# Two of twelve gate tiles add their sine product in the cosine's bank, with two ScalarE copies

## The chip, the cores and the metric

The kernel runs on one core of a Trainium2 chip. The metric is the device time of one launch in microseconds (us); lower is better. Engines are named as in the profile: PE is TensorE (PEld its weight loads), DVE is VectorE, ACT is ScalarE, POOL is GpSimd, and SP issues most of the transfers.

## The reference

```python
def _attn_ref(x):                       # x: (8, 3008, 256) float32
    X = np.fft.fft(x, axis=1)
    X = np.fft.fft(X, axis=2)
    return X.real.astype(np.float32)

def _moe_ref(x, w_gate, w_val, w_out):  # w_gate, w_val: (256, 1536), w_out: (1536, 256)
    gate = np.maximum(x @ w_gate, 0.0)
    val = x @ w_val
    return (gate * val @ w_out).astype(np.float32)
```

The real part of a two-dimensional Fourier transform of each of 8 batches (over 3008 positions and 256 channels) goes through a gated network: relu of the gate product, times the value product, times the output weights. The output is (24064, 256) in float32.

## The kernel before

**The mathematics.** The transform over the channels is folded into the weights: `WA` holds cosine combinations of the weights' rows and `WB` sine combinations (index 0 for the gate, 1 for the value). The transform over positions gives two matrices per batch, `U` (even part) and `V` (odd part), with one column for each pair of positions that mirror each other. For such a pair the gate is `WA·U + WB·V` at one position and `WA·U − WB·V` at the mirrored one; the same holds for the value. `WM` is `WB` times −2, so that adding `WM·V` to a bank that holds the sum turns it into the difference (the "mirror" matmul). Channel 128 does not fit into the 128 rows of the contraction. Its value stands in row 0 of `V`, and as a whole row in `CB`, spread over all partitions; row 0 of `WB` holds its weights, and row 0 of `WM` is zero. For the gates of batches 1 to 7 its term is therefore put into the bank ahead of the matmul by ScalarE: `CB` times a weight per partition, `b2`.

**Tiles and slots.** Batches 1 to 7 have three column blocks each (512, 512 and 481 columns), and each block has 12 tiles, one for each group of 128 of the 1536 features. A tile is a gate and a value for 128 features and one block of columns. The function `slot` emits the work of one tile step; it has tiles at four stages in hand: `pending` (the tile before), `cur`, `nxt` two tiles after `cur`, and `after` three tiles after it (the tile between, `mid`, waits). In a slot the kernel before emits:

- `sine_part(nxt)`: a matmul `WM[0]·V` into bank `g` (line 1015), and a ScalarE copy of it, `q`, to SBUF (line 1018);
- five of the eight output matmuls of the column block before (line 781; 128 × 256 each);
- `cosine_part(nxt)`: a matmul `WA[0]·U` added to the seeded bank `p` (line 1022);
- `seed(after)`: ScalarE writes `CB` times `b2` into a bank `p` (line 1010). There are two `p` banks, so this one was used by the tile two before it and must have been read by that tile's line 1026;
- the mirror matmul of `pending`'s value (line 880) and its second product on VectorE (line 910);
- the two value matmuls of `cur` (lines 874, 875) and its first product on VectorE (line 910: relu of the gate times the value, in one instruction);
- `both(nxt)`: VectorE makes the gate `sp = p − q/2` (line 1026), GpSimd the mirrored gate `sm = sp + q` (line 1027);
- GpSimd folds of a later batch, one evacuation, one sum (line 597) where there is one, and the remaining output matmuls. Some slots end with three matmuls of the next batch's position transform (line 585): by `DFT_EVEN`, slots 0 and 2 of every six in the first two column blocks, for batches that have a next one.

**What sets the order.** The program's order on every engine is written out by hand (`manual_schedule`): the order of these calls is the order in each engine's queue. Waits between engines come from the data and from the rotation of banks and buffers: one bank `g`, two each of `p`, `v` and `o`, one `d`, and 12 SBUF buffers `r` for gates.

**Around it.** Batch 0 runs in four narrower segments with other functions (`first_tile`, `single_tile`); in its first segment steps of `weights(c)` make the remaining columns of `WA` and `WB`. `gate_128` turns row 0 of `WB[0]` into the per-partition `b2` with twelve one-column matmuls (line 836) and a VectorE copy (line 837), in segment 2. At the end of batch 0 the first two tiles of batch 1 are begun ahead of time (`prime`, `seed`, `sine_part`, `cosine_part`, `both`). One tile of batch 1 (block 0, feature 6, kind "o") takes the older way with three gate matmuls and two ScalarE relus.

Of the kernel before, what the change touches and what calls it, by code (L numbers as in the profile page):

```python
# [11 lines left out]
F32 = mybir.dt.float32  # L12
BF16 = mybir.dt.bfloat16
I32 = mybir.dt.int32
F16 = mybir.dt.float16
ALU = mybir.AluOpType
ACTF = mybir.ActivationFunctionType
# [12 lines left out]
def dram(ap, offset, pattern):  # L30
    return bass.AP(ap.tensor, offset, [list(p) for p in pattern])
# [3 lines left out]
def kernel(  # L35
# [8 lines left out]
    nc = tc.nc  # L44
    B, S, D = x.shape
    DF = moe_w_gate.shape[1]
    NF = DF // 128
# [12 lines left out]
    psD = ctx.enter_context(tc.tile_pool(name="psD", bufs=1, space=PS))  # L60
    ctx.enter_context(tc.manual_schedule())

    def single(name, shape, dt=F32, pool=const):
        return pool.tile(shape, dt, name=name, tag=name)
# [4 lines left out]
    WB = [single(f"WB{i}", [128, DF], BF16) for i in range(2)]  # L69
    WM = [single(f"WM{i}", [128, DF], BF16) for i in range(2)]  # L70
# [349 lines left out]
    def weights(c):  # L420

        f = slice(c * 512, (c + 1) * 512)

        def one(i, T, W):
            p = psO.tile([128, 512], F32, name="o", tag="o")
            for kc in range(2):
                nc.tensor.matmul(p[:], lhsT=T[:, kc, :], rhs=wr[i][c][:, kc, :], start=(kc == 0), stop=(kc == 1))
            if (i, c, W) == (0, 1, WA):
                return lambda: nc.scalar.copy(W[i][:, f], p[:])
            if (i, W) in ((1, WA), (c - 1, WB)):  # L430
                nc.vector.tensor_scalar(W[i][:, f], p[:], scalar1=1.0, op0=ALU.mult, scalar2=None)  # L431
            else:
                nc.scalar.copy(W[i][:, f], p[:])
        return [lambda i=i, T=T, W=W: one(i, T, W) for i in range(2) for T, W in ((TA, WA), (TB, WB))]
# [22 lines left out]
    for t in range(3):  # L457
        n = ROWS[1][t]
        p = slice(0, n)
# [42 lines left out]
            nc.gpsimd.tensor_tensor(FF[0][p, 0, t, :, 0:1], even[:, :, 0:1], even[:, :, 0:1], op=ALU.add)  # L502
    start_pool.__exit__(None, None, None)
    ch128 = nc.dram_tensor("ch128", (B, 4 * NJ + 1), BF16, kind="Internal").ap()
    b2 = single("b2", [128, NF])
    one = single("one", [1, 1], BF16)
    nc.vector.memset(one[:], 1.0)


    def even_table(n, c):  # L510
# [311 lines left out]
    fold_even()  # L822
    turns_and_rows()

    more = {(0, i): [s] for i, s in enumerate(weights(1) + weights(2))}
    for n, c in enumerate(even_order):
        for k, step in enumerate(even_table(n, c)):
            more.setdefault(divmod(EVEN_AT[n] + k, NF), []).append(step)
# [1 line left out]
    for seg in (2, 3):  # L830
        more.setdefault((1, 8 + seg), []).append(lambda seg=seg: minus_v(nc.scalar, seg))

    def gate_128():
        p = psD.tile([128, 512], F32, name="d", tag="d")
        for f in range(NF):
            nc.tensor.matmul(p[:, f:f + 1], lhsT=WB[0][0:1, f * 128:(f + 1) * 128], rhs=one[:], start=True, stop=True)
        nc.vector.tensor_scalar(b2[:], p[:, 0:NF], scalar1=1.0, op0=ALU.mult, scalar2=None)
    more[(2, 2)] = [gate_128]
    more_1 = {}
    for at, step in zip((-5, -4, -3, -2, -1, 7, 7, 8, 14, 17), channel_loads() + channel_turn()):  # L840
        (more_1 if at >= 0 else more).setdefault(at if at >= 0 else (3, NF + at), []).append(step)

# [4 lines left out]
    todo_out, todo_dft, todo_fold = [], [], []  # L847
    credit, paired = 0, False
    pending = None

    def run(todo, n):
        for _ in range(min(n, len(todo))):
            todo.pop(0)()
        if not paired:
            flush()

    def run_one(todo):
        if todo:
            todo.pop(0)()
# [17 lines left out]
    def mirror(bank, st, i):  # L877

        W, v = (WB, st["vm"]) if st["b"] == 0 else (WM, st["vs"])
        nc.tensor.matmul(bank[:, 0:st["n"]], lhsT=W[i][:, st["f"]], rhs=v, start=False, stop=True, skip_group_check=True)  # L880

    def bank(tag):
        return {"g": psG, "p": psP, "v": psV, "d": psD}[tag].tile([128, 512], F32, name=tag, tag=tag)

    def space():
        return rp.tile([128, 512], F32, name="r", tag="r", bufs=12)

    def relu(st):
        st["r"] = space()
        nc.scalar.activation(st["r"][:, 0:st["n"]], st["g"][:, 0:st["n"]], ACTF.Relu)  # L890
# [6 lines left out]
    def mult(st, sign, r=None):  # L897
        n = st["n"]
        nc.vector.tensor_tensor(half_h(st, sign), (r or st["r"])[:, 0:n], st["v"][:, 0:n], op=ALU.mult)  # L899
# [8 lines left out]
    def relu_mult(st, sign):  # L908
        n = st["n"]
        nc.vector.scalar_tensor_tensor(half_h(st, sign), in0=st["s"][1 + sign][:, 0:n], scalar=0.0, in1=st["v"][:, 0:n],  # L910
                                       op0=ALU.max, op1=ALU.mult)

    def second(st):
        (relu_mult if "s" in st else mult)(st, 1)
        if st["n"] == 481:
            keep_rest(st)
# [5 lines left out]
    def value(st):  # L922
        st["v"] = bank("v")
        two(st["v"], st, 1)

    def gate(st, tag="g"):
        st["g"] = bank(tag)
        two(st["g"], st, 0)
        relu(st)
# [10 lines left out]
    def single_tile(st, outs, extra=(), last=(), tag="p"):  # L940

        gate(st, tag)
        if pending is not None:
            finish(pending)
        value(st)
        mult(st, 0)
        run(todo_out, outs)
        for step in extra:
            step()
        mirror(st["g"], st, 0)  # L950
        relu(st)
        run(todo_out, outs)
        for step in last:
            step()
        return st

    def first_tile(st, extra, outs):
# [31 lines left out]
    def new_tiles():  # L989
        for b in range(1, B):  # L990
            for blk, block in enumerate(thirds):
                for fi in range(NF):
                    st = tile_of(block, fi, uv[b])
                    st["b"] = b
                    st["kind"] = "o" if (b, blk, fi) == (1, 0, 6) else "n"
                    st["lead"] = (b, blk, fi) == (1, 0, 0)
                    yield st

    def prime():
# [4 lines left out]

    def seed(st, p=None):

        if st is None or st["kind"] == "o":
            return
        st["p"] = p or bank("p")
        nc.scalar.activation(st["p"][:, 0:st["n"]], st["c"], ACTF.Copy, scale=b2[:, st["fi"]:st["fi"] + 1])  # L1010

    def sine_part(st):
        n = st["n"]
        st["g"] = bank("g")
        nc.tensor.matmul(st["g"][:, 0:n], lhsT=WM[0][:, st["f"]], rhs=st["vs"], start=True, stop=True)  # L1015
        q = space()
        st["s"] = q, space(), q
        nc.scalar.copy(q[:, 0:n], st["g"][:, 0:n])  # L1018

    def cosine_part(st):  # L1020
        n = st["n"]
        nc.tensor.matmul(st["p"][:, 0:n], lhsT=WA[0][:, st["f"]], rhs=st["us"], start=False, stop=True, skip_group_check=True)  # L1022

    def both(st):
        n, (q, sp, sm) = st["n"], st["s"]
        nc.vector.scalar_tensor_tensor(sp[:, 0:n], in0=q[:, 0:n], scalar=-0.5, in1=st["p"][:, 0:n], op0=ALU.mult, op1=ALU.add)  # L1026
        nc.gpsimd.tensor_tensor(sm[:, 0:n], sp[:, 0:n], q[:, 0:n], op=ALU.add)  # L1027

    def slot(cur, mid, nxt, after, outs, fold_us):

        stop = len(todo_out)

        def out(part):
            run(todo_out, len(todo_out) - stop + outs * part // 8)
        old = nxt is not None and nxt["kind"] == "o"
        new = nxt is not None and not old
        if old:
            gate(nxt)
        lead = cur["lead"]
        if lead:  # L1040
            out(5)
        if new and mid["kind"] != "o":
            sine_part(nxt)
        out(3 if not lead else 5)
        out(5)
        if new and mid["kind"] == "o":
            sine_part(nxt)
        if new:
            cosine_part(nxt)
        seed(after)  # L1050
        if pending is not None:
            mirror(pending["v"], pending, 1)
        if pending is not None:
            second(pending)
        value(cur)
        if cur["kind"] == "o":
            mult(cur, 0, cur["first"])
        else:
            relu_mult(cur, 0)
        if new:  # L1060
            both(nxt)
        if old:
            nxt["first"] = nxt["r"]
            mirror(nxt["g"], nxt, 0)
            relu(nxt)
        run_fold(fold_us)
        run_one(evict)
        run_one(sums)
        out(8)
        return cur  # L1070
# [4 lines left out]
    for b in range(B):  # L1075
# [4 lines left out]
        for blk, block in enumerate(blocks):  # L1080
# [44 lines left out]
            if (b, blk) == (0, 0):  # L1125
                for fi in range(NF):
                    st = tile_of(block, fi, (U, V, CB))
                    add_h(st, hs)
                    if fi == 8:
                        todo_out = out_steps(b, block, hs, True)  # L1130
                    pending = first_tile(st, more.get((0, fi), ()), 6)
                mirror(pending["g"], pending, 0)
                relu(pending)
            elif not paired:
                for fi in range(NF):
                    st = tile_of(block, fi, (U, V, CB))
                    add_h(st, hs)
                    tag = {(3, 8): "g", (3, 9): "d", (3, 10): "g", (3, 11): "d"}.get((blk, fi), "p")
# [8 lines left out]
                    if (blk, fi) == (1, 8):  # L1147
                        run(todo_out, len(todo_out))
                        todo_out = out_steps(b, block, hs, True)
                    pending = single_tile(st, 3 if blk == 1 else per_tile // 2, more_b.get((blk, fi), ()), last, tag)  # L1150
                    run(todo_dft, DFT_0[blk - 1][fi])
            else:
                for fi in range(NF):
                    at = NF * blk + fi
                    cur = ahead.pop(0)
# [17 lines left out]
            if (b, blk) == (B - 1, 2):  # L1173
                todo_out = rest
# [38 lines left out]
```

## Time and profile before

| | us |
|---|---|
| median of 3 runs | 630.92 |
| lowest, highest | 630.84, 631.08 |
| the profiled execution | 630.98 |
| its span in the trace | 629.2 |
| busy: PE, DVE, ACT, POOL | 620.5, 551.5, 445.5, 502.7 |

The page names groups of instructions by the line of the kernel, the engine, the operation, and what is written from what. Ends of matmuls are modelled, because matmuls are pipelined: a 512-column matmul shows about 0.38 us although the next one starts 0.22 us later. Distances between starts are therefore the better measure on TensorE. A row of the timeline has the start, the duration (of all merged instructions, with their count at the end), and in brackets the engine's idle time ahead of it with its releaser. The clock of TensorE was granted in full all along.

### The profile page before, as it was taken

The numbers are of one execution on the slowest core, as the hardware profiler recorded it, in microseconds if no ns is written. First come the engines' busy times: TensorE is split into PE (matmuls) and PEld (weight loads), VectorE is DVE, ScalarE is ACT, GpSimd is POOL, SyncE is SP. The second block draws the span as 40 slices with busy tenths as digits, with TensorE's granted clock in tenths as the row PEclk, the third lists the DMA queues.
The fourth block names the chain that finished last, engine by engine and source line by source line (L and its number), as shares of the span: only waits on it lengthen the run. The fifth ranks groups of instructions, "written<-read, shape, count | busy, mean of one in ns | idle before, by whom it ended". The sixth has DMA issues, their size and how long they took to land.

```text
span 629.2 us, 12441 instructions
## 1 busy us (share of the span) xinstructions
PE 620.5 (99%) x4114; PEld 398.4 (63%) x4114; DVE 551.5 (88%) x981; ACT 445.5 (71%) x813; POOL 502.7 (80%) x478
## 2 busy tenths in 40 slices
PE   8999999999999999999999999999999999999997
PEld 2566666566666666666666666666666666666666
DVE  8886676999899899988999999899999989999991
ACT  7796667777777767777777777777777777777762
POOL 8887992898999988799979989699886566666660
PEclk9999999999999999999999999999999999999999
DMA  9953748734264327315362426211221111211113
GB/s 240 209 206 118 173 177 102 182 73 151 82 150 145 126 76 183 113 44 165 83 187 64 140 76 130 68 50 36 77 61 38 42 60 56 57 38 51 51 44 102
DMA packets 82911, 66.47 MB, mean 106 GB/s; under 512 B 38517, under 2 KB 65941, under 8 KB 82846
## 3 DMA queue, kind: packets, MB, share of 16 engines
q1 hardware_dynamic: 78260, 60.01, 34.3%
q0 software_dynamic: 3984, 4.92, 3.9%
q10 hardware_dynamic: 602, 0.75, 0.4%
q8 instruction: 32, 0.52, 0.4%
q14 instruction: 33, 0.27, 0.2%
HBM read 41.88 MB, written 34.16 MB: 121 GB/s over the span
## 4 chain that ended last, share of the span: by engine, by line
PE 91%; DVE 4%; issue 2%; POOL 1%; DMA 1%; ACT 1%; DVEq 0%; ACTq 0%; POOLq 0%
PE o L781 36%; PE v L880 10%; PE v L875 9%; PE v L874 9%; PE g L1015 8%; PE p L1022 8%; PE d L585 4%; DVE h L910 2%; PE p L880 1%; PE p L874 1%; PE p L875 1%; DMA XG<-in_x_dram,gidx 1%; DVE h L899 1%; DVE r L1026 1%; POOL XG L120 1%
## 5 line engine op out<-in xcount | busy, mean ns | idle before, releaser
L1027 POOL TENSOR_TENSOR r<-r 128x512 f32<-128x512 f32 (+1 forms) x251 | 313.2, 1254 | 100.5 <-DVE r L1026 98.1
L910 DVE SCALAR_TENSOR_TENSOR h<-r,v 128x512 bf16<-128x512 f32 (+1 forms) x502 | 317.1, 673 | 39.2 <-PE v L880 26.5
L781 PE MATMUL o<-wo,h 128*128 128x256 bf16 x2172 | 330.6, 272 | 0.0
L781 PEld LDWEIGHTS <-h 128*128 128x128 bf16 x2220 | 216.7, 98 | 112.0 <-issue 1.3
L1010 ACT ACTIVATE p<-CB,b 128x512 f32<-128x512 bf16 (+1 forms) x251 | 171.8, 684 | 73.4 <-DVE r L1026 72.1
L1018 ACT COPY r<-g 128x512 f32<-128x512 f32 (+1 forms) x251 | 145.1, 578 | 66.5 <-PE g L1015 57.4
L1026 DVE SCALAR_TENSOR_TENSOR r<-r,p 128x512 f32<-128x512 f32 (+1 forms) x251 | 167.9, 669 | 0.9 <-ACT r L1018 0.9
L875 PE MATMUL v<-V,WB 128*128 128x512 bf16 (+3 forms) x296 | 108.6, 367 | 0.0
L874 PE MATMUL v<-U,WA 128*128 128x512 bf16 (+3 forms) x296 | 108.6, 367 | 0.0
L880 PE MATMUL v<-V,WM 128*128 128x512 bf16 (+1 forms) x252 | 94.4, 375 | 0.8 <-DVE h L910 0.4
L1015 PE MATMUL g<-V,WM 128*128 128x512 bf16 (+1 forms) x251 | 94.1, 375 | 0.5 <-ACT r L1018 0.4
L1022 PE MATMUL p<-U,WA 128*128 128x512 bf16 (+1 forms) x251 | 94.1, 375 | 0.2 <-ACT p L1010 0.2
L899 DVE TENSOR_TENSOR h<-r,v 128x376 bf16<-128x376 f32 (+2 forms) x90 | 46.2, 546 | 17.6 <-PE v L880 10.1
L874 PEld LDWEIGHTS <-WA 128*128 128x128 bf16 x348 | 33.9, 97 | 39.5 <-issue 10.4
L875 PEld LDWEIGHTS <-WB 128*128 128x128 bf16 x348 | 34.0, 98 | 34.3 <-DVE WB L431 0.6
L794 ACT COPY os<-o 128x512 f32<-128x512 f32 x92 | 52.6, 571 | 3.5 <-issue 3.0
L198 POOL TENSOR_TENSOR XG<-XG,XD 128x510 f32<-128x510 f32 x42 | 53.0, 1270 | 0.8 <-DMA XG<-xr 0.8
L890 ACT ACTIVATE r<-p 128x376 f32<-128x376 f32 (+1 forms) x80 | 38.0, 486 | 17.8 <-PE p L880 9.0
L206 POOL TENSOR_TENSOR AA<-XG 128x510 f32<-128x510 f32 x42 | 45.5, 1093 | 0.0
L1015 PEld LDWEIGHTS <-WM 128*128 128x128 bf16 x251 | 24.6, 98 | 5.7 <-issue 0.3
L1022 PEld LDWEIGHTS <-WA 128*128 128x128 bf16 x251 | 24.5, 98 | 3.7 <-issue 0.8
L880 PEld LDWEIGHTS <-WM 128*128 128x128 bf16 x253 | 24.8, 98 | 3.1
(186 smaller groups left out, 412.3 us busy)
## 6 DMA issues: line engine op xcount, KB each, us to landing
out_dram<-os SPq DMA_DIRECT2D x124, 128.0 KB
xr<-in_x_dram SPq DMA_DIRECT2D x12, 768.0 KB
XG<-xr SPq DMA_DIRECT2D x12, 768.0 KB
XD<-in_x_dram SPq DMA_DIRECT2D x15, 512.0 KB
out_dram<-os SPq DMA_DIRECT2D x35, 112.0 KB
XD<-in_x_dram SPq DMA_DIRECT2D x8, 448.0 KB
CB<-ch SPq DMA_DIRECT2D x7, 376.2 KB
out_dram<-os SPq DMA_DIRECT2D x13, 96.0 KB
```

What stands on the lines that cost most here:

```text
L198: e.tensor_tensor(XG[p, r, t, ::-1, 1:D], XG[p, r, t, ::-1, 1:D], XD[p, r, t, :, D - 1:0:-1], op=ALU.add)
L781: nc.tensor.matmul(st["p"][0:m, q, :], lhsT=lhs(f), rhs=wo[:, f, :], start=(f == 0 and not (early and q)), stop=(f == NF - 1), skip_group_ ...
L874: nc.tensor.matmul(bank[:, 0:st["n"]], lhsT=WA[i][:, st["f"]], rhs=st["us"], start=True, stop=False)
L875: nc.tensor.matmul(bank[:, 0:st["n"]], lhsT=WB[i][:, st["f"]], rhs=st["vs"], start=False, stop=True)
L880: nc.tensor.matmul(bank[:, 0:st["n"]], lhsT=W[i][:, st["f"]], rhs=v, start=False, stop=True, skip_group_check=True)
L910: nc.vector.scalar_tensor_tensor(half_h(st, sign), in0=st["s"][1 + sign][:, 0:n], scalar=0.0, in1=st["v"][:, 0:n], op0=ALU.max, op1=ALU.mult)
L1010: nc.scalar.activation(st["p"][:, 0:st["n"]], st["c"], ACTF.Copy, scale=b2[:, st["fi"]:st["fi"] + 1])
L1015: nc.tensor.matmul(st["g"][:, 0:n], lhsT=WM[0][:, st["f"]], rhs=st["vs"], start=True, stop=True)
L1018: nc.scalar.copy(q[:, 0:n], st["g"][:, 0:n])
L1022: nc.tensor.matmul(st["p"][:, 0:n], lhsT=WA[0][:, st["f"]], rhs=st["us"], start=False, stop=True, skip_group_check=True)
L1026: nc.vector.scalar_tensor_tensor(sp[:, 0:n], in0=q[:, 0:n], scalar=-0.5, in1=st["p"][:, 0:n], op0=ALU.mult, op1=ALU.add)
L1027: nc.gpsimd.tensor_tensor(sm[:, 0:n], sp[:, 0:n], q[:, 0:n], op=ALU.add)
```

## The change

- **Copied tiles.** In batches 1 to 7, features 2 and 8 of every column block (in batch 1's first block, features 5 and 9) get a new way. When such a tile is `nxt`, the slot emits no sine matmul for it; the seed of `after` is emitted first, then the cosine matmul, then `copy_cosine`: ScalarE copies twice the bank to SBUF. One slot later, when the tile is `mid`, `add_sine` adds `WB[0]·V` to the same bank, behind the sine matmul of that slot's own `nxt`; ScalarE copies the sum as the gate, and GpSimd subtracts: twice the cosine part minus the sum is the mirrored gate. VectorE has no line 1026 for such a tile.
- **Row 0 of `WB[0]`.** Since `add_sine` uses `WB[0]` with a seeded bank, its row 0 is overwritten with the zero row of `WM[0]` by a transfer after the first slot of batch 1.
- **`b2` by transfers.** `gate_128` goes. SP writes row 0 of `WB[0]` to memory (segment 1, feature 1) and reads it back one element per descriptor across partitions (segment 1, feature 4); ScalarE copies it to `b2` where `gate_128` stood.
- **The old tile goes.** Every tile of batches 1 to 7 has the new ways.
- **Batch 1's first slot.** Its order becomes: half of the outputs, the sine matmul, the pending tile's mirror and the value matmuls, the rest of the outputs to five eighths, then the cosine matmul, the seed and `both`. At the end of batch 0, evacuations that are due in the last tile are emitted after the steps that begin batch 1, not ahead of them.
- **Batch 0's weights.** The steps of `weights(2)` come one tile earlier (features 3 to 6 instead of 4 to 7).

```diff
+    wrow = nc.dram_tensor("wrow", (1, DF), BF16, kind="Internal").ap()
     b2 = single("b2", [128, NF])
-    one = single("one", [1, 1], BF16)
-    nc.vector.memset(one[:], 1.0)
+    brow = single("brow", [128, NF], BF16)
...
-    more = {(0, i): [s] for i, s in enumerate(weights(1) + weights(2))}
+    more = {(0, i): [s] for i, s in enumerate(weights(1))}
+    for i, step in enumerate(weights(2)):
+        more.setdefault((0, 3 + i), []).append(step)
...
-    def gate_128():
-        p = psD.tile([128, 512], F32, name="d", tag="d")
-        for f in range(NF):
-            nc.tensor.matmul(p[:, f:f + 1], lhsT=WB[0][0:1, f * 128:(f + 1) * 128], rhs=one[:], start=True, stop=True)
-        nc.vector.tensor_scalar(b2[:], p[:, 0:NF], scalar1=1.0, op0=ALU.mult, scalar2=None)
-    more[(2, 2)] = [gate_128]
-    more_1 = {}
+    def keep_128():
+        nc.sync.dma_start(out=wrow, in_=WB[0][0:1, :])
+
+    def get_128():
+        nc.sync.dma_start(out=brow[:], in_=dram(wrow, 0, [[1, 128], [128, NF]]), allow_slow_non_contiguous=True)
+    more[(1, 1)].append(keep_128)
+    more[(1, 4)].append(get_128)
+    more[(2, 2)] = [lambda: nc.scalar.copy(b2[:], brow[:])]
+    more_1 = {0: [lambda: nc.sync.dma_start(out=WB[0][0:1, :], in_=WM[0][0:1, :])]}
...
-        run(todo_out, outs)
+        for _ in range(outs):
+            run_one(todo_out)
         for step in last:
             step()
+        run(todo_out, 0)
...
-                    st["kind"] = "o" if (b, blk, fi) == (1, 0, 6) else "n"
                     st["lead"] = (b, blk, fi) == (1, 0, 0)
+                    st["copied"] = fi in (2, 8) and (b, blk) != (1, 0) or (b, blk, fi) in ((1, 0, 5), (1, 0, 9))
...
+    def copy_cosine(st):
+
+        n, sp, sm = st["n"], space(), space()
+        st["s"] = sm, sp, sm
+        nc.scalar.mul(sm[:, 0:n], st["p"][:, 0:n], 2.0)
+
+    def add_sine(st):
+        n, (_, sp, sm) = st["n"], st["s"]
+        nc.tensor.matmul(st["p"][:, 0:n], lhsT=WB[0][:, st["f"]], rhs=st["vs"], start=False, stop=True, skip_group_check=True)
+        nc.scalar.copy(sp[:, 0:n], st["p"][:, 0:n])
+        nc.gpsimd.tensor_tensor(sm[:, 0:n], sm[:, 0:n], sp[:, 0:n], op=ALU.subtract)
+
     def slot(cur, mid, nxt, after, outs, fold_us):
...
+        copied = nxt is not None and nxt["copied"]
+        if cur["lead"]:
+            out(4)
+        if nxt is not None and not copied:
+            sine_part(nxt)
+        if mid is not None and mid["copied"]:
+            add_sine(mid)
+        if cur["lead"]:
+            rest_of_pending()
+            value_of_cur()
+            out(5)
+            cosine_part(nxt)
+            seed(after)
+            both(nxt)
+        else:
+            out(5)
+            if copied:
+                seed(after)
+                cosine_part(nxt)
+                copy_cosine(nxt)
+            elif nxt is not None:
+                cosine_part(nxt)
+                seed(after)
+            rest_of_pending()
+            value_of_cur()
+            if nxt is not None and not copied:
+                both(nxt)
```

In the kernel after, the copy of the cosine part is line 1038, the added sine matmul line 1042, the copy of the sum line 1043 and GpSimd's subtraction line 1044.

More of the change, by code (lines that the diff above doesn't have):

```diff
@@ L1005, in seed @@
     def seed(st, p=None):
[L1007 to L1010, printed above, removed]
+        if st is not None:
+            st["p"] = p or bank("p")
+            nc.scalar.activation(st["p"][:, 0:st["n"]], st["c"], ACTF.Copy, scale=b2[:, st["fi"]:st["fi"] + 1])
     def sine_part(st):
@@ L1034, in out, with rest_of_pending, value_of_cur @@
             run(todo_out, len(todo_out) - stop + outs * part // 8)
[L1035 to L1040, printed above, removed]
-            out(5)
[L1042 to L1048, printed above, removed]
-            cosine_part(nxt)
[L1050 to L1057, printed above, removed]
-        else:
[L1059 to L1065, printed above, removed]
+        def rest_of_pending():
+            if pending is not None:
+                mirror(pending["v"], pending, 1)
+                second(pending)
+        def value_of_cur():
+            value(cur)
+            relu_mult(cur, 0)
+        copied = nxt is not None and nxt["copied"]
[8 more added lines that the diff above has]
+            value_of_cur()
+            out(5)
+            cosine_part(nxt)
+            seed(after)
+            both(nxt)
+        else:
+            out(5)
[10 more added lines that the diff above has]
+                both(nxt)
         run_fold(fold_us)
```

## The prediction

> **What bounds the kernel now.** I read the page's first part, then stage windows and the list of waits, then the timeline at the places where the new work goes.
>
> ```profile
> span 629.2 us, 12441 instructions
> PE 620.5 (99%) x4114; PEld 398.4 (63%) x4114; DVE 551.5 (88%) x981; ACT 445.5 (71%) x813; POOL 502.7 (80%) x478
> ```
>
> ```profile
> 280.00:350.00 70.00, 69.90 (x462) 44.99 (x461) 64.72 (x111) 51.18 (x89) 62.02 (x54) 1.00 0.41 118
> ```
>
> ```profile
> ACT p L1010 <- DVE r L1026: 72.1, 197, 0.7
> ```
>
> The second fence is the windows view (PE, PEld, DVE, ACT, POOL, granted clock). TensorE is busy for 69.90 of 70 us at clock 1.00, so from batch 1 on a slot costs its matmuls, and every new TensorE wait is paid in full. VectorE is next at 64.72. The third fence says that ScalarE's seed (line 1010) waits in 197 slots for VectorE's line 1026, which frees the seed's bank.
>
> Now one pair of slots in column block 0 of batch 5: TensorE, VectorE, ScalarE.
>
> ```profile
> 411.24 0.49 PE L781 MATMUL o<-wo,h 128*128 128x256 bf16 x3
> 411.57 0.38 PE L1015 MATMUL g<-V,WM 128*128 128x512 bf16 x1
> 411.79 0.71 PE L781 MATMUL o<-wo,h 128*128 128x256 bf16 x5
> 412.33 0.38 PE L1022 MATMUL p<-U,WA 128*128 128x512 bf16 x1
> 412.62 0.38 PE L880 MATMUL v<-V,WM 128*128 128x512 bf16 x1
> ...
> 413.26 0.49 PE L781 MATMUL o<-wo,h 128*128 128x256 bf16 x3
> 413.59 0.64 PE L585 MATMUL d<-tabC,F 128*128 128x376 bf16 x3
> 414.07 0.38 PE L1015 MATMUL g<-V,WM 128*128 128x512 bf16 x1
> 414.29 0.71 PE L781 MATMUL o<-wo,h 128*128 128x256 bf16 x5
> 414.84 0.38 PE L1022 MATMUL p<-U,WA 128*128 128x512 bf16 x1
> ```
>
> ```profile
> 411.03 0.34 DVE L597 SCALAR_TENSOR_TENSOR V<-es,d 128x188 bf16<-128x188 f32 x1
> 411.29 1.27 DVE L910 SCALAR_TENSOR_TENSOR h<-r,v 128x512 bf16<-128x512 f32 x2
> 412.49 0.68 DVE L1026 SCALAR_TENSOR_TENSOR r<-r,p 128x512 f32<-128x512 f32 x1
> ```
>
> ```profile
> 413.20 0.69 ACT L1010 ACTIVATE p<-CB,b 128x512 f32<-128x512 bf16 x1 [0.57 <-DVE r L1026]
> 413.83 0.58 ACT L794 COPY os<-o 128x512 f32<-128x512 f32 x1
> ```
>
> Ends of matmuls are modelled, so I use start to start: a 512-column matmul takes 0.22 us (414.07 to 414.29), three output matmuls 0.33 (411.24 to 411.57), five 0.54 to 0.55, three transform matmuls 0.48 (413.59 to 414.07). The mirror at 412.62 starts 0.29 after the cosine matmul instead of 0.22: it waits 0.07 for the two line-910 products (411.29 plus 1.27 is 412.56), since they read the bank that it adds to. Line 1026 of that slot starts only at 412.49, and the seed at 413.20, as it ends. So a seed runs late in its slot (413.20 to 413.89); today that harms nobody, since its consumer is the cosine matmul of the next slot, at 414.84.
>
> **The change, part by part.**
>
> *Copied tiles in the steady state.* Two tiles in twelve, 6 a batch, 42 in all. TensorE's work is equal: one cosine and one sine matmul. VectorE loses 42 of line 1026 (0.68 each, 28 us), ScalarE gains 42 copies (about 0.58 each, 24 us), GpSimd keeps its one operation, which now waits for ScalarE; it is needed only two slots later, and costs nothing. What that is worth depends on which engine bounds. By the rows, outputs follow each other at 0.11 us (0.33 for three) and wide matmuls at 0.22 with no gap but the 0.07 above: TensorE bounds, and the 28 us off VectorE buy only such gaps.
>
> The Trainium skill (Perfetto Trace Analysis, "Identifying the Most-Contended Engine") says that matmul busy time is a poor measure of how close TensorE is to its limit, and that the share of weight loading is a better one, while for VectorE occupancy serves. By that rule TensorE stands at 63% and VectorE at 88% here, and relief of VectorE would be worth up to its 28 us; the sum below would then end near 601 instead of 652. The trace does not bear it out: the matmuls' starts leave no room for it.
>
> The order, though, moves two things. The sine matmul leaves the slot of the cosine and goes to the start of the next slot, behind that slot's own sine matmul; and it adds to the bank that the new copy reads, so it must wait for that copy. The copy is queued on ScalarE behind the seed, and the seed behind VectorE.
>
> Put into the rows above, the copied tile's cosine belongs to the slot of 412.33. Without the 411.57 matmul the outputs run from 411.57 and the cosine at 412.12; the mirror could start at 412.34 but its VectorE releaser is unchanged, so it stays at 412.62: the 0.22 taken from this slot are lost in waiting. From there 413.26, 413.59 and 414.07 (next tile's sine) stand as they are, and the copied tile's sine matmul is due at 414.29. ScalarE: the seed still starts at 413.20, the next instruction can start at 413.83, as the row of line 794 shows, now the copy, which ends at about 414.42; TensorE follows some 0.05 later, at 414.47. That is 0.18 late. Five outputs later the next cosine starts at 414.47 + 0.22 + 0.54 = 415.23 instead of 414.84: +0.39 for this tile.
>
> Where no transform matmuls stand in between, their 0.48 of cover is gone. Column block 2 of batch 3, by engine again:
>
> ```profile
> 310.43 0.49 PE L781 MATMUL o<-wo,h 128*128 128x256 bf16 x3
> 310.76 0.37 PE L1015 MATMUL g<-V,WM 128*128 128x481 bf16 x1
> 310.96 0.71 PE L781 MATMUL o<-wo,h 128*128 128x256 bf16 x5
> 311.51 0.37 PE L1022 MATMUL p<-U,WA 128*128 128x481 bf16 x1
> ...
> 313.40 0.37 PE L1022 MATMUL p<-U,WA 128*128 128x481 bf16 x1
> ```
>
> ```profile
> 310.30 1.23 DVE L910 SCALAR_TENSOR_TENSOR h<-r,v 128x481 bf16<-128x481 f32 x2
> 311.44 0.65 DVE L1026 SCALAR_TENSOR_TENSOR r<-r,p 128x481 f32<-128x481 f32 x1
> ```
>
> ```profile
> 310.23 0.67 ACT L1010 ACTIVATE p<-CB,b 128x481 f32<-128x481 bf16 x1 [0.34 <-DVE r L1026]
> 310.83 0.58 ACT L794 COPY os<-o 128x512 f32<-128x512 f32 x1
> 311.31 0.56 ACT L1018 COPY r<-g 128x481 f32<-128x481 f32 x1
> 312.12 0.67 ACT L1010 ACTIVATE p<-CB,b 128x481 f32<-128x481 bf16 x1 [0.25 <-DVE r L1026]
> ```
>
> A matmul is 0.20 here (310.76 to 310.96). Cosine at 311.31, mirror at 311.58 (line 910 ends at 311.53), two value matmuls and three outputs to 312.52, the next sine, the copied tile's sine due at 312.72. ScalarE: seed at 312.12, copy from 312.72 (0.60 later, as 310.23 to 310.83) for 0.56 to 313.28, TensorE at 313.32: 0.60 late. The next cosine comes at 313.32 + 0.20 + 0.55 = 314.07 instead of 313.40: +0.67.
>
> The other places follow from these two. The row of line 597 at 411.03 pushes VectorE back by 0.26 in the two slots ahead of most of these places; where it does not, the first place gives about 0.25 instead of 0.39, and without transform matmuls 0.25 + 0.48 = 0.73. Sum:
> - 17 tiles like the first (feature 8 of column block 0 in batches 2 to 6, both of block 1 in batches 1 to 6): 17 × 0.39 = 6.6
> - 5 with transforms and no lag (feature 2 of block 0, batches 2 to 6): 5 × 0.25 = 1.3
> - 2 in batch 1 (features 5 and 9), between 0.25 and 0.73, taken as 0.5: 1.0
> - 6 at the seam to block 2 (feature 2), with lag and no transforms: 0.39 + 0.48 less 0.03 for the narrower matmuls = 0.84, together 5.0
> - 6 of feature 8 in block 2: 6 × 0.67 = 4.0
> - batch 7, which has no next batch to transform: 4 × 0.73 + 2 × 0.67 = 4.3
>
> That is 22.2 us of new TensorE time. Bounds: nothing, if the copy were always in time; at most 42 × 0.87 = 37, if every place had the lag and no transforms. I take the sum, since each place has its own row.
>
> *One old tile goes* (batch 1, feature 6): three matmuls become two, −0.2. ScalarE's second relu with it is off the path.
>
> *Row of weights by transfers.* The twelve one-column matmuls go:
>
> ```profile
> 64.29 0.45 PE L836 MATMUL d<-one,WB 1*128 1x1 bf16 x12
> 64.67 0.33 PE L880 MATMUL p<-CB,WB 128*128 128x376 bf16 x1
> ```
>
> −0.4 (64.29 to 64.67). In their place stand three SP transfers: the row to memory, 1536 single elements back, and one row into WB before batch 1's first copied tile; and a small ScalarE copy in the slot of 64.29, behind which the relus of batch 0 queue. The nearest transfer rows are these of 4-byte elements:
>
> ```profile
> L133 SPq DMA_DIRECT2D CX<-in_x_dram x8: 618/1326/8454, 94.9 to 132.7; - x8
> ```
>
> An issue of 0.6 to 8.5 us, some ten slots ahead of need: hidden, taken as 0; up to +4 if it comes late, since SP's output transfers stand behind it and the ScalarE queue behind the copy.
>
> *Batch 1's entry.* The sequence before:
>
> ```profile
> 104.53 0.59 ACT L794 COPY os<-o 128x512 f32<-128x512 f32 x1
> 105.00 0.62 ACT L1018 COPY r<-g 128x512 f32<-128x512 f32 x1
> ```
>
> ```profile
> 104.74 0.49 PE L781 MATMUL o<-wo,h 128*128 128x256 bf16 x3
> 105.66 0.38 PE L1015 MATMUL g<-V,WM 128*128 128x512 bf16 x1 [0.44 <-ACT r L1018]
> 106.25 0.38 PE L1022 MATMUL p<-U,WA 128*128 128x512 bf16 x1 [0.21 <-ACT p L1010]
> ```
>
> The evacuation at 104.53 delays the copy, and the copy the matmul at 105.66. Now the evacuation comes after, so the copy starts about 0.3 earlier, and the finishing and value matmuls fill the gap ahead of 106.25: −0.7, between 0 and the two waits of 0.60 and 0.37, start to start, −1.0. The second weight steps, one tile earlier in batch 0, reorder equal work: 0, within ±0.3.
>
> Sum: 22.2 − 0.2 − 0.4 − 0.7 = +20.9. The profiled execution took 630.98 us (span 629.2 and 1.8 around it), 0.06 over the median of 630.92; 630.92 + 20.9 gives 651.8.
>
> **Rivals.**
>
> *Faster: VectorE's relief decides.* If the copies always ended before the sine matmul is due, which needs 0.18 us less at the first place and 0.60 at the second, nothing new is paid; the 0.07 waits such as at 412.62, some four a batch and larger ones elsewhere, would go for about 2 us, with the 1.3 above: 627.6. For it: VectorE is 92% busy in the window (64.72 of 70). Against it: line 1026 is dropped one slot after the one that the seed waits for. Chance 0.09.
>
> *Much faster: VectorE bounds.* Then its 42 × 0.68 = 28 us come off the span: 630.9 − 1.3 − 28 = 601.6. For it, VectorE's 88%; against it, matmuls that start every 0.11 and 0.22 us without a gap. Chance 0.02. This is the rule named above, of the Trainium skill's page Perfetto Trace Analysis.
>
> *Only the uncovered places pay.* Where transforms stand between, the miss is only 0.18, and a slightly earlier seed closes it. Then 5.0 + 4.0 + 4.3 − 1.3 = +12.0: 642.9. Chance 0.15.
>
> *ScalarE falls behind as well.* In the slot after the copied one it has two copies, a seed and an evacuation, 2 × 0.48 (310.83 to 311.31) + 0.63 (413.20 to 413.83) + 0.48 = 2.1 us beside a slot of about 2.2. If the next sine copy is late by 0.1 each time, 42 × 0.1 = 4.2 more: 656. Chance 0.08. A late transfer (up to +4) ends there as well.
>
> *No measurable change*, gains and waits cancelling: 0.03.
>
> **How the numbers follow.** The forecast has 0.63. With the rivals of the uncovered places and of a late ScalarE, slower holds 0.86, same 0.03, faster 0.11; 0.2%, or 1.3 us, is about what a measurement of this kernel tells from no change. The forecast's own range is 646 to 656 (0.1 us per tile either way); widened to take in 642.9 and 656 with as much around them, 639 to 658 leaves out less than 2 in 10.
>
> **What would show it.** The new sine matmul (42 times, line 1042) would have TensorE idle before it, released by ScalarE's line 1038; start to start about 0.2 us where transforms precede and 0.6 elsewhere. The mirror after a copied tile's cosine would start later after it than 0.22. VectorE's busy time falls by about 28 us, ScalarE's rises by about 24, and TensorE's share falls. I am wrong if line 1038 starts before the seed's VectorE releaser ends, or if the 42 matmuls follow their neighbours at 0.22.

## The result, and the profile after

The changed kernel takes 651.46 us (median of 4 runs, 651.22 to 651.72) against 630.95 of the kernel before: a ratio of 1.0325, with a 95% interval of 1.0307 to 1.0343. It is slower by 20.5 us; the forecast was 20.9. The profiled execution took 651.44 us, with a span of 649.7. One of the ten runs of the version without copied tiles, further below, took 2299 us, for a reason that nothing here shows, and its ratio leaves that run out.

From the page of the kernel after, the span, the busy times and the chain that ended last:

```profile
span 649.7 us, 12395 instructions
PE 629.1 (97%) x4101; PEld 397.6 (61%) x4101; DVE 525.8 (81%) x938; ACT 460.1 (71%) x856; POOL 504.6 (78%) x479
...
PE 61%; DVE 24%; issue 8%; ACT 3%; DMA 2%; POOL 1%; DVEq 0%; SPq 0%; ACTq 0%; POOLq 0%
```

The same chain on the page of the kernel before:

```profile
PE 91%; DVE 4%; issue 2%; POOL 1%; DMA 1%; ACT 1%; DVEq 0%; ACTq 0%; POOLq 0%
```

No engine has more to do in proportion to its time: every busy share is the same as in the kernel before or lower. What changed is the chain: TensorE's share in it fell from 91% to 61%, and VectorE's rose from 4% to 24%. TensorE now follows VectorE and ScalarE at 42 places. Grouped by line (busy time, mean, idle time ahead of the group with its releaser):

```profile
L1042 PE MATMUL p<-V,WB 128*128 128x512 bf16 (+1 forms) x42 | 15.6, 372 | 8.9 <-ACT r L1038 8.8
L884 PE MATMUL v<-V,WM 128*128 128x512 bf16 (+1 forms) x252 | 94.3, 374 | 4.3 <-DVE h L914 2.1
```

Since the modelled ends of matmuls cover up to 0.16 us of each wait, I measured distances between starts over the whole trace, less the distance that is kept where nothing waits (0.216 us behind 512 columns, 0.203 behind 481), and counted what is over 0.03 us. By this measure the 42 new sine matmuls (line 1042) wait 15.7 us in all. The mirror matmuls from the first tiles of batch 1 on (line 880, now 884) waited 5.1 us before and wait 11.7 us now. Together that is 22.3 us of new waiting; the prediction's sum for the copied tiles was 22.2.

The place of the prediction's first rows (column block 0 of batch 5), on TensorE, ScalarE and VectorE:

```profile
422.07 1.04 PE L781 MATMUL o<-wo,h 128*128 128x256 bf16 x8
422.94 0.38 PE L1027 MATMUL p<-U,WA 128*128 128x512 bf16 x1
423.45 0.38 PE L884 MATMUL v<-V,WM 128*128 128x512 bf16 x1
...
424.42 0.64 PE L585 MATMUL d<-tabC,F 128*128 128x376 bf16 x3
424.90 0.38 PE L1020 MATMUL g<-V,WM 128*128 128x512 bf16 x1
425.29 0.38 PE L1042 MATMUL p<-V,WB 128*128 128x512 bf16 x1
425.50 0.71 PE L781 MATMUL o<-wo,h 128*128 128x256 bf16 x5
```

```profile
424.03 0.69 ACT L1015 ACTIVATE p<-CB,b 128x512 f32<-128x512 bf16 x1 [1.36 <-DVE r L1031]
424.65 0.58 ACT L1038 ACTIVATE r<-p 128x512 f32<-128x512 f32 x1
```

```profile
422.12 1.27 DVE L914 SCALAR_TENSOR_TENSOR h<-r,v 128x512 bf16<-128x512 f32 x2
423.31 0.68 DVE L1031 SCALAR_TENSOR_TENSOR r<-r,p 128x512 f32<-128x512 f32 x1
```

The eight outputs now stand together, since the sine matmul between them has gone. The mirror starts 0.51 after the cosine instead of 0.22: it waits for the products of line 914, which end at 423.39. ScalarE stands idle for 1.36 us ahead of the seed, until line 1031 ends at 423.99, and the copy (line 1038) follows 0.62 later and ends at 425.23. The sine matmul starts at 425.29, 0.39 after its neighbour instead of 0.22. Both waits have the size that the prediction worked out (the mirror's from 0.07 to about 0.28, the sine matmul's 0.18; here 0.29 and 0.17).

And the second kind, block 2 of batch 3, where no transforms stand in between:

```profile
323.28 0.37 PE L1020 MATMUL g<-V,WM 128*128 128x481 bf16 x1
324.10 0.36 PE L1042 MATMUL p<-V,WB 128*128 128x481 bf16 x1 [0.45 <-ACT r L1038]
```

```profile
322.89 0.67 ACT L1015 ACTIVATE p<-CB,b 128x481 f32<-128x481 bf16 x1 [1.22 <-DVE r L1031]
323.49 0.55 ACT L1038 ACTIVATE r<-p 128x481 f32<-128x481 f32 x1
```

0.82 between the starts instead of 0.20: 0.62 late, against 0.60 in the prediction.

### The profile page after: what moved, and what is told of

It reads as the page before. It is cut to its first block, busy times and chain, and to the rows that moved or that the text cites. A ratio compares the mean times of both kernels' runs of the same rounds, so it can differ in the third digit from the quotient of the medians.

```text
span 649.7 us, 12395 instructions
## 1 busy us (share of the span) xinstructions
PE 629.1 (97%) x4101; PEld 397.6 (61%) x4101; DVE 525.8 (81%) x938; ACT 460.1 (71%) x856; POOL 504.6 (78%) x479
## 4 chain that ended last, share of the span: by engine, by line
PE 61%; DVE 24%; issue 8%; ACT 3%; DMA 2%; POOL 1%; DVEq 0%; SPq 0%; ACTq 0%; POOLq 0%
PE o L781 22%; DVE h L914 16%; PE v L884 7%; DVE r L1031 7%; PE v L879 5%; PE v L878 5%; PE p L1027 5%; PE g L1020 4%; PE d L585 4%; PE p L1042 2%; ACT r L1038 2%; PE p L884 1%; DMA XG<-xr 1%; PE p L878 1%; DMA XG<-in_x_dram,gidx 1%
## 5 line engine op out<-in xcount | busy, mean ns | idle before, releaser
L781 PE MATMUL o<-wo,h 128*128 128x256 bf16 x2172 | 324.7, 272 | 0.0
L1023 ACT COPY r<-g 128x512 f32<-128x512 f32 (+1 forms) x210 | 121.6, 579 | 42.4 <-PE g L1020 37.7
L1031 DVE SCALAR_TENSOR_TENSOR r<-r,p 128x512 f32<-128x512 f32 (+1 forms) x210 | 140.5, 669 | 0.6 <-ACT r L1023 0.6
L1020 PE MATMUL g<-V,WM 128*128 128x512 bf16 (+1 forms) x210 | 78.8, 375 | 0.1
L1044 POOL TENSOR_TENSOR r<-r 128x512 f32<-128x512 f32 (+1 forms) x42 | 52.6, 1253 | 22.3 <-ACT r L1043 22.3
L903 DVE TENSOR_TENSOR h<-r,v 128x376 bf16<-128x376 f32 (+1 forms) x88 | 44.6, 542 | 17.4 <-PE v L884 8.8
L884 PEld LDWEIGHTS <-WM 128*128 128x128 bf16 x252 | 24.7, 98 | 2.9
```

What stands on the lines that cost most here:

```text
L781: nc.tensor.matmul(st["p"][0:m, q, :], lhsT=lhs(f), rhs=wo[:, f, :], start=(f == 0 and not (early and q)), stop=(f == NF - 1), skip_group_ ...
```

## The experiments

The theory: one chain from the mirror matmul of the slot before (VectorE's products, line 1031, the seed, the copy) sets the earliest start of the added sine matmul, and the sine matmul's absence from the first slot adds a wait at the mirror. The rivals: ScalarE is late because of its load; the copy costs something wherever it stands; the two waits are separate losses; VectorE's relief is worth something that the waits hide.

### The copy ahead of the seed

```diff
             if copied:
-                seed(after)
                 cosine_part(nxt)
                 copy_cosine(nxt)
+                seed(after)
```

> In the copied slots the cosine matmul and its ScalarE copy are emitted ahead of the seed, everything else as after. Theory of the chain (VectorE product, seed, copy, added sine matmul): the copy no longer stands behind the seed, so the 42 waits of the added sine matmul (15.7 us start to start in the trace of after) go, and the mirror matmul's waits stay: 651.5 - 15.7 = 635.8 us. Rival that ScalarE is late because of its load (one more copy in a slot), whatever the order: within 2 us of 651.5.

Measured: 635.65 us (635.58 to 635.85), 1.0075 times the kernel before [1.0058, 1.0092], 15.8 us less than after. In its trace, TensorE and ScalarE at a place of the first kind:

```profile
427.43 0.38 PE L1027 MATMUL p<-U,WA 128*128 128x512 bf16 x1
427.93 0.38 PE L884 MATMUL v<-V,WM 128*128 128x512 bf16 x1
...
429.39 0.38 PE L1020 MATMUL g<-V,WM 128*128 128x512 bf16 x1
429.61 0.38 PE L1042 MATMUL p<-V,WB 128*128 128x512 bf16 x1
```

```profile
427.90 0.60 ACT L1038 ACTIVATE r<-p 128x512 f32<-128x512 f32 x1 [0.76 <-PE p L1027]
428.51 0.69 ACT L1015 ACTIVATE p<-CB,b 128x512 f32<-128x512 bf16 x1
```

The copy now starts 0.47 after the cosine matmul that it waits for, and is done at 428.50, more than a microsecond before its consumer, which follows its neighbour at 0.22. The seed comes at 428.51, after the copy, and nobody is late for it (the cosine matmuls, its consumers, wait 0.1 us in the whole trace). The same instructions, in another order, take 15.7 us of waiting away: ScalarE's load is not the cause. The mirror's waits are as in after (11.6 us; 0.50 after the cosine here).

### Seven outputs ahead of the cosine

```diff
-            out(5)
+            out(7 if copied else 5)
             if copied:
```

> In the copied slots seven outputs instead of five are emitted ahead of the cosine matmul (and so one instead of three at the end), in the place of the sine matmul that has gone; the seed stays ahead of the copy. If the mirror's wait and the added sine matmul's wait are two ends of one chain that starts at the mirror of the slot before, the first goes and the second grows by as much: 651.5 us, within 1. If they are two separate losses, the mirror's 6.6 us (11.7 in after, 5.1 in before) are saved: 644.9 us.

Measured: 651.43 us (651.19 to 651.58), the same as after. Its trace on TensorE:

```profile
422.88 0.38 PE L1027 MATMUL p<-U,WA 128*128 128x512 bf16 x1
423.16 0.38 PE L884 MATMUL v<-V,WM 128*128 128x512 bf16 x1
...
424.40 0.38 PE L1020 MATMUL g<-V,WM 128*128 128x512 bf16 x1
425.00 0.38 PE L1042 MATMUL p<-V,WB 128*128 128x512 bf16 x1 [0.22 <-ACT r L1038]
```

The mirror stands 0.28 after the cosine again, and the sine matmul is 0.60 after its neighbour instead of 0.39. Over the trace the mirror's waits fall from 11.7 to 5.2 us and the sine matmul's rise from 15.7 to 22.2: what is given at one end is taken at the other, and the sum stays. So as long as the copy stands behind the seed, the two waits are one loss, set by the chain's length and by the matmuls that TensorE has in between.

### Both

```diff
-            out(5)
+            out(7 if copied else 5)
             if copied:
-                seed(after)
                 cosine_part(nxt)
                 copy_cosine(nxt)
+                seed(after)
```

> Both edits: the copy ahead of the seed, and seven outputs ahead of the cosine matmul. Theory of the chain: no new wait is left, 651.5 - 15.7 - 6.6 = 629.2 us; with VectorE's relief worth nothing, the same as without copied tiles. If VectorE's relief is worth its part of the mirror's waits, about 2 us less: 627 us.

Measured: 629.58 us (629.21 to 629.97), a ratio of 0.9977 [0.9968, 0.9987]. The sine matmul waits nowhere, and the mirrors wait 5.2 us, against 5.1 before the change.

### No copied tiles

```diff
-                    st["copied"] = fi in (2, 8) and (b, blk) != (1, 0) or (b, blk, fi) in ((1, 0, 5), (1, 0, 9))
+                    st["copied"] = False
```

> No tile is copied; the transfers of the weights' row, the removed old tile and the new order at the start of batch 1 stay. The prediction's credit by itself: 0.4 for the twelve small matmuls, 0.7 for the start of batch 1, 0.2 for the old tile, 630.9 - 1.3 = 629.6 us. If a transfer of a single-element row comes late, up to 634 us.

Measured: 629.89 us, a ratio of 0.9983 [0.9974, 0.9993]. The credit of the rest of the change is 1.1 us against the 1.3 of the prediction. The transfers hide: the row's way back issues in 0.39 us, and the copy to `b2`, some 17 us later, finds it there (on the run's list of groups ScalarE has no idle time ahead of it).

```profile
L839 SPq DMA_DIRECT2D brow<-wrow x1: 394/394/394, 45.8 to 45.8; - x1
L842 ACT CAST b<-brow x1: 192/192/192, 63.4 to 63.4; 128x12 f32<-128x12 bf16 x1
```

At batch 1's entry, from the first sine matmul to the one of batch 1's second slot, it takes 106.46 − 102.53 = 3.93 us, and took 107.87 − 103.26 = 4.61 before: 0.68 less (predicted 0.7).

Beside the run with both edits, this one shows that VectorE's relief is worth 0.3 us at these places: the two kernels differ in 42 products moved from VectorE (526.7 against 551.1 us busy), and the intervals of their ratios to the kernel before overlap. The mirrors wait 5.8 us here and 5.2 there.

This kernel has all of the change but the copied tiles, so it is also the base for what they cost. The kernel after takes 21.6 us more and has 21.6 us more of these waits (15.7 and 11.7, less 5.8); the copy ahead of the seed 5.8 us more, with 5.8 of waits; seven outputs 21.5 us more, with 21.6. To 0.1 us the two kinds of waits account for the time.

### Features 0 and 6 instead of 2 and 8

```diff
-                    st["copied"] = fi in (2, 8) and (b, blk) != (1, 0) or (b, blk, fi) in ((1, 0, 5), (1, 0, 9))
+                    st["copied"] = fi in (0, 6) and (b, blk) != (1, 0) or (b, blk, fi) in ((1, 0, 5), (1, 0, 9))
```

> As after, but the copied tiles are features 0 and 6 instead of 2 and 8 (batch 1's first block keeps 5 and 9), so the slot of their cosine and the one after it have no transform matmuls between the mirror and the added sine matmul. Theory of the chain: every place pays what the places without transforms pay, 0.73 us in the wide blocks (27 tiles) and 0.67 in the narrow one (13), about 1.0 for the other two, less 1.3: 630.9 + 19.7 + 8.7 + 1.0 - 1.3 = 659 us. If the loss belongs to the copy itself (one more ScalarE instruction, contention), wherever it stands: 651.5 us.

Measured: 655.53 us (655.28 and 655.77), a ratio of 1.0386 [1.0367, 1.0405]. The cost depends on the place, as the theory says, but it is 3.5 us under the number. The sine matmuls wait 26.4 us, 0.65 in the wide blocks and 0.61 in the narrow one, near what was counted for them. (26 of the places are in the wide blocks and 14 in the narrow one, not 27 and 13, which moves the expectation by 0.1 us.) What the expectation left out is the other side: the mirrors wait 5.3 us in all, about as before the change (5.1), though they wait at 40 of the 42 copied places, most of them 0.05 to 0.2 us and together 4.1. So most of the old waits at the other mirrors have gone. The reason would be that VectorE now loses its product just where it has the sums as well; the next two runs take this alone.

### Both edits, with the copied tiles where VectorE is late

```diff
-            out(5)
+            out(7 if copied else 5)
             if copied:
-                seed(after)
                 cosine_part(nxt)
                 copy_cosine(nxt)
+                seed(after)
...
-                    st["copied"] = fi in (2, 8) and (b, blk) != (1, 0) or (b, blk, fi) in ((1, 0, 5), (1, 0, 9))
+                    st["copied"] = fi in (0, 6) and (b, blk) != (1, 0) or (b, blk, fi) in ((1, 0, 5), (1, 0, 9))
```

The second run has (5, 11) in place of (0, 6).

> The copy ahead of the seed and seven outputs ahead of the cosine, with the copied tiles at features 0 and 6: VectorE loses its gate product in the slots where it also does the sums (line 597). If VectorE's relief is worth something only where VectorE is late, about 3 of the 5.2 us of the mirror's waits go: 626.6 us. If it is worth nothing anywhere: 629.6 us. If the copy's chain still bites where no transforms stand: above 631.

> As the run before, with the copied tiles at features 5 and 11, one slot earlier in each period (the slot of the first sum). Same theory: about 626.6 us if relief pays where VectorE is late, 629.6 if it pays nowhere.

Measured: 627.83 us (627.31 to 628.17), a ratio of 0.9947 [0.9933, 0.9960], and 627.84 us (627.74 to 628.16), 0.9949 [0.9935, 0.9963]. VectorE in the run with both edits and features 2 and 8, where two sums push it back:

```profile
407.65 0.34 DVE L597 SCALAR_TENSOR_TENSOR V<-es,d 128x188 bf16<-128x188 f32 x1
407.91 1.27 DVE L914 SCALAR_TENSOR_TENSOR h<-r,v 128x512 bf16<-128x512 f32 x2
409.11 0.68 DVE L1031 SCALAR_TENSOR_TENSOR r<-r,p 128x512 f32<-128x512 f32 x1
409.70 0.34 DVE L597 SCALAR_TENSOR_TENSOR V<-es,d 128x188 bf16<-128x188 f32 x1
409.96 1.27 DVE L914 SCALAR_TENSOR_TENSOR h<-r,v 128x512 bf16<-128x512 f32 x2
```

And in the run with features 0 and 6:

```profile
406.10 0.68 DVE L1031 SCALAR_TENSOR_TENSOR r<-r,p 128x512 f32<-128x512 f32 x1
406.70 0.34 DVE L597 SCALAR_TENSOR_TENSOR V<-es,d 128x188 bf16<-128x188 f32 x1
406.96 1.28 DVE L914 SCALAR_TENSOR_TENSOR h<-r,v 128x512 bf16<-128x512 f32 x2
408.16 0.34 DVE L597 SCALAR_TENSOR_TENSOR V<-es,d 128x188 bf16<-128x188 f32 x1
408.81 1.28 DVE L914 SCALAR_TENSOR_TENSOR h<-r,v 128x512 bf16<-128x512 f32 x2 [0.31 <-PE v L884]
```

The second sum stands where a product of line 1031 would have been, and VectorE is idle for 0.31 us ahead of the next slot's products, where it ran without a pause in the rows above. The mirrors' waits fall from 5.2 us to 3.0 and 2.5. The gain over features 2 and 8 is 1.75 us, rather more than half of the 3 that were expected. These are the fastest versions here, about 0.5% under the kernel before.

## Why the prediction was right

- **What bounds.** That TensorE's matmuls have no room between them, and VectorE's 28 us are therefore worth only the gaps that they close, held: with the order mended, taking 24 us of busy time off VectorE changed the time by 0.3 us (629.58 and 629.89). For TensorE the Trainium skill (Perfetto Trace Analysis, "Identifying the Most-Contended Engine") names two measures in place of busy time, the matmul work done against the peak and the share of weight loading. The prediction went by the second alone; by that alone VectorE would have been the bound, and no run agrees with that. The first was not worked out here. The page is right that matmul busy time doesn't tell: TensorE showed 97% in a kernel that lost 22.3 us in waiting. Distances between starts told.
- **The steady state.** The sum of 22.2 us came out at 22.3, and not because errors cancel: in the order of the prediction's list its terms of 6.6, 1.3, 1.0, 5.0, 4.0 and 4.3 us measured 6.5, 1.5, 0.9, 4.8, 4.1 and 4.3. At single places: 0.17 for 0.18 at the sine matmul with transforms in between, 0.62 for 0.60 in the narrow block, 0.65 plus 0.05 to 0.09 at the mirror for 0.73 in the wide blocks of batch 7. The chain's order (VectorE, seed, copy, sine matmul) is shown by the swap, which took away 15.8 us, and that the two waits are its two ends by the seven outputs, which changed nothing. The signs of being wrong did not occur: the copy follows the seed at all 42 places and starts after the seed's releaser has ended, and none of the 42 matmuls follows its neighbour at 0.22.
- **A step of which only the size was off.** ScalarE's busy time was to rise by 24 us and rose by 14.6 (445.5 to 460.1). The added instructions do take that long (line 1038 23.9 and line 1043 25.1 us, against 23.5 less of the line that was 1018), but busy time counts overlapping instructions once, and the new copies stand back to back with others (424.03, 424.65). Added up one by one, the durations on ScalarE rose by 24.7 us. VectorE's busy time fell by 25.7 us, and its durations by 28.6, where 28 was forecast. Neither has weight in the time.
- **The rest.** Batch 1's entry gave 0.68 of 0.7, the whole credit 1.1 of 1.3, and the transfers were hidden.
- **The rivals.** "VectorE's relief decides" fell, since TensorE waited at every one of the 42 places. So did "only the uncovered places pay": places with transforms pay too, by 0.16 to 0.18 at the sine matmul beside the mirror's part. "ScalarE falls behind" is ruled out by the swap, and the sine matmuls that it would have delayed (line 1020) wait 0.4 us in the whole trace of after. But the first of them had a true size in it: its 627.6 us is met within 0.3 (627.83 and 627.84) once the copy stands ahead of the seed, seven outputs ahead of the cosine, and the tiles are chosen where VectorE has its sums, not two slots later.

## What to carry to other kernels

An instruction moved to an engine with time to spare lands at a place in that engine's queue, and its latency is that of the wait ahead of it: look at what the instruction before it waits for, not at the engine's share. When a matmul is taken out of one slot and put into the next, count what it had covered in the first. And relieve a second engine in the slot where it is late; the same relief two slots later bought 0.3 us here, against about 2.

## What was not expected

- Two waits that look like separate losses in the profile were one: 6.5 us were taken from the mirrors' waits (11.7 to 5.2) and came back in full at the sine matmuls (15.7 to 22.2): 651.43 us against 651.46.
- The transfer that gathers 1536 single 2-byte elements issued in 0.39 to 0.57 us over the eight traces that have it (0.39 in six), less than any of the eight transfers of 4-byte elements by which it was bounded (0.62 to 8.45 us).
